# Light token groups as whole alternative slot bodies, and a later output table, in an attention + mixture-of-experts kernel

## The chip, the core and the metric

The kernel runs on one core of a Trainium2 chip. The metric is the device time of one execution in microseconds (us). The engines are called by the names the profile uses: PE (TensorE, matrix products), DVE (VectorE), ACT (ScalarE), POOL (GpSimd), and SP (SyncE, which issues most of the DMA transfers). Each engine has its own instruction stream; streams meet at semaphores.

## What is computed

Three stages follow each other. The reference, cut to what matters:

```python
attn = softmax(mask(q @ k.T / 8))            # batch 2, 12 heads, 448 positions, head size 64, causal
x    = merge_heads(attn @ v)                 # 896 tokens x 768
logits = unit(x) @ unit(expert_emb).T / tau  # 8 experts; one expert per token (argmax)
for e in range(8):                           # w1[e]: 768x1024, w2[e]: 1024x768
    h = relu(x[mask_e] @ w1[e])
    out[mask_e] = gate[mask_e] * (h @ w2[e])
h = maximum(maximum(out @ W1, out @ W2), out @ W3)   # three 768x768 matrices
y = h @ w_out                                        # 768x768
```

How many tokens fall to each expert is known only while the kernel runs. With the inputs that are timed the eight counts are 58, 5, 0, 109, 283, 0, 96 and 345.

## The kernel before, in words

**Stages.** Attention runs until about 122 us of the profiled execution. Routing is mixed into the end of attention: DVE counts the tokens of each expert, and small matrix products turn the counts into places. Then come the expert slots, up to 12 of them. A *heavy* slot computes 128 tokens of one expert (operands are split into a high and a low half in fp32r, and high by high, high by low and low by high are multiplied). With the counts above there are seven heavy slots, 0 to 6: expert 4 in slots 0 and 1, expert 6 in slot 2, expert 7 in slots 3, 4 and 5, expert 3 in slot 6. What is left of an expert (at most 64 tokens) is a *light* group; it is computed beside a heavy slot that needs no new weights, as a rider. Here expert 4's rest (27 tokens) rides in slot 3, expert 0's 58 in slot 4, expert 1's 5 in slot 6. Slot 5 has no rider. After the slots come the product with three matrices and maximum (345 to 471 us), then the output product (to 514 us), whose rows are scattered by an indirect DMA with the index table `sidx`.

**A slot.** `slot(i)` issues, on PE: L1 (768 to 1024, halves `l1[0]`, `l1[1]`), the transposes of the previous slot's result (`ytr`), transposes of the hidden layer (`htr`), L2 in four pieces, and the transposes of the next slot's gathered tokens (`xnext`). Interleaved with these, `S.ws` splits the next slot's weights: ACT casts the raw tile to the high half (L250), DVE subtracts for the low half (L251), both inside `tc.If(self.need > 0)`, since only a change of expert needs it. The raw tiles are DMAs on SP (768 KB each, six buffers). Slots 1, 2 and 5 prepare a new expert's weights.

**Tables.** The placement of the light groups is worked out on DVE with small operations: `lights1` (placed in slot 0 by a written order, the token `lt1`), `lights2` and `lights3` (between the routing and the middle of slot 1), then `light_gates` and `sorted_table` (in slot 1, the token hook `(1, 0)`), which builds the one-hot operand for the 16 small products `ix` that PE does at the end of slot 1, and `sidx`. The integer table `tabi` holds what the engines load into registers: offsets, whether weights are new, the number of slots (T_N), and for each light group its size, expert and offset.

**A light rider.** `Light` has five parts (`x`, `L1`, `hT`, `L2`, `out`), each in units of 32 tokens. Every unit stands in a conditional block of its own on every engine (`tc.If(self.n > 32 * u)` at L410, `tc.If(self.n > 0)` at L402 and L416), nine conditional blocks for each slot from 3 on. L1 uses four column tiles of 32 (one per 256 of the 1024 columns), L2 three of 32.

**Control.** Slots 3 to 11 are nested in `tc.If(nslot > i)` (L1212). `mark_branch_hint_location` at the end of a slot tells PE, POOL and SP ahead of time which way the next of these tests will go. Behind the nest stands a second test for tail groups (`ntail`, L1217), whose body is jumped over here.

## Time and profile before

| | us |
|---|---|
| three timed runs | 522.18, 525.52, 525.69 |
| median | 525.52 |
| profiled execution | 521.98 |
| its span (first to last instruction) | 520.3 |

| stretch of the profiled execution | from | to |
|---|---|---|
| attention, routing | 0 | 122 |
| slot 0, slot 1 (start of its L1) | 122 | 142.8 |
| slot 1 | 142.8 | 172.4 |
| slot 2 | 173.0 | 195.3 |
| slot 3, with a rider of 27 tokens | 195.3 | 225.6 |
| slot 4, with a rider of 58 tokens | 225.6 | 263.0 |
| slot 5, no rider | 263.0 | 290.3 |
| slot 6, with a rider of 5 tokens | 290.3 | 325.2 |
| no PE work | 325.2 | 334.9 |
| three matrices, maximum | 334.9 | 471 |
| output product and last stores | 471 | 520.3 |

Slot boundaries are the first L1 product of each slot on PE. PE is busy for 90% of the span, so a view is read by asking where PE idles and who ends that idle time. "PEclk" in a row is the TensorE clock that was granted, as a share of full speed.

### The profile page before, as it was taken

The page shows a single profiled execution, that of the slowest core. Times are in us where ns is not written, and L with a number is a line of the kernel's source. Part 1 is how long each engine was busy: PE and PEld are TensorE (multiplying, and loading weights), DVE is VectorE, ACT ScalarE, POOL GpSimd, SP SyncE. Part 2 cuts the span into 40 slices and gives each one's busy share as a digit, 9 for nine tenths or more (in the row PEclk, how much of TensorE's full clock was granted, in tenths as well). Part 3 has the DMA queues.
Part 4 walks back from the last instruction along what each step waited for, and adds up shares of the span by engine and source line. Part 5 has one row for each costly group of instructions (what it writes and reads, how often), then busy time and mean ns, then how long its engine had stood idle before and what let it go on. Part 6 is the DMA issues. An engine that isn't in the chain of part 4 may idle for free. (4 is left out here: it accounts for less than half of the span.)

```text
span 520.3 us, 9113 instructions
## 1 busy us (share of the span) xinstructions
PE 470.7 (90%) x2968; PEld 396.9 (76%) x2968; DVE 310.9 (60%) x707; ACT 236.9 (46%) x521; POOL 47.7 (9%) x80
## 2 busy tenths in 40 slices
PE   7999999998795899989987789299999999999995
PEld 6756666776785698777876568289999999999994
DVE  5898878985769875101014711269998898941000
ACT  6668679895454485122043631253444444321000
POOL 5321121110101020100001000000000000000111
PEclk9999999999897799999999789699999999999998
DMA  8645239610266699682416953643443550000111
GB/s 226 213 126 142 78 91 371 225 37 19 61 227 248 235 330 350 230 325 68 149 61 186 398 197 129 245 186 118 170 142 118 181 174 9 1 0 31 62 60 61
DMA packets 28652, 81.72 MB, mean 157 GB/s; under 512 B 13432, under 2 KB 14968, under 8 KB 28576
## 3 DMA queue, kind: packets, MB, share of 16 engines
q1 hardware_dynamic: 25648, 71.46, 39.3%
q0 software_dynamic: 2304, 9.24, 5.3%
q8 instruction: 31, 0.51, 0.4%
q14 instruction: 45, 0.37, 0.2%
q10 hardware_dynamic: 624, 0.14, 0.2%
HBM read 75.33 MB, written 5.51 MB: 155 GB/s over the span
## 5 line engine op out<-in xcount | busy, mean ns | idle before, releaser
L1177 PE MATMUL pm<-x2h,dwl 128*128 128x448 f32 x204 | 74.7, 366 | 0.0
L1176 PE MATMUL pm<-x2l,dwh 128*128 128x448 f32 x204 | 74.7, 366 | 0.0
L1175 PE MATMUL pm<-x2h,dwh 128*128 128x448 f32 x204 | 74.6, 365 | 0.0
L622 PE MATMUL pss<-kt,qbd 128*128 128x320 f32 (+6 forms) x168 | 45.7, 395 | 0.9 <-ACT prb L636 0.6
L1181 PE MATMUL l<-w2h,hh 128*128 128x384 f32 x112 | 41.1, 367 | 3.3 <-PEq L410 2.2
L636 ACT ACTIVATE prb<-pss,sm 128x64 f32<-128x64 f32 (+6 forms) x84 | 39.5, 483 | 9.6 <-DVE sm L629 9.4
L251 DVE TENSOR_TENSOR w1l<-raw,w1h 128x768 fp32r<-128x768 f32 x24 | 21.8, 953 | 34.6 <-ACT w1h L250 30.5
L1181 PE MATMUL l<-w2l,hh 128*128 128x384 f32 x112 | 39.2, 350 | 2.9 <-DVE w2l L270 2.9
L1176 PEld LDWEIGHTS pm<-x2l,dwh 128*128 128x128 f32 x204 | 38.3, 188 | 3.3
L1175 PEld LDWEIGHTS pm<-x2h,dwh 128*128 128x128 f32 x204 | 38.3, 188 | 3.3
L1177 PEld LDWEIGHTS pm<-x2h,dwl 128*128 128x128 f32 x204 | 38.3, 188 | 3.3
L183 ACT CAST dwh<-dt_t 128x768 fp32r<-128x768 f32 (+1 forms) x20 | 15.5, 773 | 48.0 <-DVE dt_t L182 48.0
L1181 PE MATMUL l<-w2h,hl 128*128 128x384 f32 x112 | 28.4, 357 | 9.7 <-DVE hl L213 5.6
L1181 PE MATMUL l<-w1h,xhp 128*128 128x512 f32 x73 | 33.1, 453 | 3.6 <-ACT w1h L250 1.5
L622 PEld LDWEIGHTS pss<-kt,qbd 128*128 128x128 f32 x168 | 28.1, 190 | 9.3 <-issue 1.7
L629 DVE TENSOR_REDUCE sm<-pss 128x1 f32<-128x448 f32 (+6 forms) x84 | 31.4, 412 | 4.6 <-PE pss L625 4.4
L1181 PE MATMUL l<-w1l,xhp 128*128 128x512 f32 x73 | 31.6, 433 | 0.0
L656 PE MATMUL pst<-ident,prb 128*128 128x128 f32 x192 | 30.0, 281 | 1.8 <-DVE prb L646 1.4
L1181 PEld LDWEIGHTS l<-w2h,hl 128*128 128x128 f32 x112 | 21.4, 199 | 10.5 <-DVE hl L213 6.0
L1177 PE MATMUL po<-woh,h2l 128*128 128x384 f32 (+2 forms) x84 | 28.1, 335 | 0.0
L1176 PE MATMUL po<-wol,h2h 128*128 128x384 f32 (+2 forms) x84 | 28.1, 334 | 0.0
L1175 PE MATMUL po<-woh,h2h 128*128 128x384 f32 (+2 forms) x84 | 28.1, 334 | 0.0
(329 smaller groups left out, 953.4 us busy)
## 6 DMA issues: line engine op xcount, KB each, us to landing
raw<-in_moe_w_dram SPq DMA_DIRECT2D x56, 768.0 KB, 6.5
rawd<-in_moe_w_dram SPq DMA_DIRECT2D x18, 768.0 KB, 4.4
rawd<-in_moe_w_out_dram SPq DMA_DIRECT2D x6, 768.0 KB, 4.2
vr<-in_v_dram SPq DMA_DIRECT2D x12, 256.0 KB, 2.8
kt<-in_k_dram SPq DMA_DIRECT2D x12, 224.0 KB, 3.5
xd<-xall POOLq DMA_DIRECT2D x12, 224.0 KB, 3.3
qbd<-in_q_dram SPq DMA_DIRECT2D x23, 112.0 KB, 4.1
xrp<-xd,idx POOLq DMA_INDIRECT x8, 7.4
```

Source lines behind the costliest of these rows:

```text
L183: nc.scalar.copy(out=hi[:, c0:c1], in_=f)
L251: nc.vector.tensor_tensor(out=lo[:, sl], in0=r[:, sl], in1=hi[:, sl], op=ALU.subtract)
L622: nc.tensor.matmul(ps[:, o:o + n], lhsT=qbd[p % 4][:, i], rhs=ktt[p][:, :n], start=i == SG[g][0], stop=False, skip_group_check=True)
L629: nc.vector.tensor_reduce(out=sms[p][:, 0, SC[i]:SC[i] + 1], in_=held["s", p, g][:, SO[i]:SO[i] + 64 * (i + 1)], axis=AX.X, op=ALU.max, ne ...
L636: nc.scalar.activation(out=prb[p % 2][:, poff[i]:poff[i] + n], in_=ps[:, SO[i]:SO[i] + n], func=AF.Exp, bias=sm[:, 0, SC[i]:SC[i] + 1], sc ...
L656: nc.tensor.transpose(ps[:, n * P:(n + 1) * P], prb[p % 2][:, poff[i] + kt * P:poff[i] + (kt + 1) * P], ident)
L1175: nc.tensor.matmul(o, lhsT=lh, rhs=rh, start=first, stop=False)
L1176: nc.tensor.matmul(o, lhsT=lh, rhs=rl, start=False, stop=False)
L1177: nc.tensor.matmul(o, lhsT=ll, rhs=rh, start=False, stop=last)
L1181: nc.tensor.matmul(o, lhsT=a, rhs=b, start=first and n == 0, stop=last and n == len(ops) - 1)
```

## The change

Six things are changed together.

1. A slot from 3 on is one of three whole bodies, chosen by a number `kind` (two bits for each slot in one register): no rider, a rider of up to 32 tokens, a rider of up to 64 tokens. Each body is straight: the rider's parts have no conditional blocks of their own, and a body with a rider has no weight preparation.
2. The rider's shapes: 32 tokens use four column tiles of 32 in L1 and in L2, 64 tokens two column tiles of 64 in both.
3. The placement tables have fewer DVE operations. `lights1` becomes `lights` and stands later (behind `qh1` in the written order); `lights2` and `lights3` become one `lights2`, which stands in slot 2 behind the last split of w1 and ahead of those of w2. `light_bases` (two operations) follows at the end of slot 2. `light_gates` is gone.
4. At the end of slot 2 every engine loads T_KIND into a register.
5. The tail groups are tested ahead of the slots 3 to 11, with a hint, instead of behind them; the hints for the next slot's test are now also given to ACT and DVE, in bodies with a rider, from the test of slot 4 on.
6. `sorted_table` and its 16 products stand behind the three-matrix stage.

The diff, cut to these parts:

```diff
     class Light:
-        def __init__(self, s, raw_of=None):
...
-        def units(self, part):
-            for u in range(2):
-                with tc.If(self.n > 32 * u):
-                    part(u)
+        def __init__(self, row, nt):
+            self.row, self.nt, self.T = row, nt, P // nt
+            self.w = {}
...
+            self.load([(0, p) for p in (0, 2, 1, 3)])
+            nc.gpsimd.tensor_copy(out=lix, in_=idx[:, bass.ds(self.e + NH, 1)])
+            nc.gpsimd.indirect_dma_start(out=lxr[:nt], out_offset=None, in_=xd, in_offset=bass.IndirectOffsetOnAxis(ap=lix[:nt], axis=0))
+            nc.gpsimd.tensor_copy(out=lgt, in_=grep[:, self.T // 4, bass.ds(self.e, 1)])
+            self.load([(1, p) for p in (0, 2)])
...
         def L1(self):
+            T, f = self.T, 1024 // self.T
+            for k in range(KD):
+                for t in range(T):
+                    n, c0 = divmod(t * f, 512)
+                    w = self.w[0, 2 * n + k // 3].rearrange("p (k f) -> p k f", k=3)
+                    self.mm(pb, self.xT[:, k], w[:, k % 3, c0:c0 + f], k, t, f, k == KD - 1)
...
     def slot(i, prep, prev):
         S = Slot(i, prep)
         S.begin()
         S.regs()
-        R = S.rider = Light(i, S.raw_of) if i > 2 else None
+        if i < 3:
+            slot_body(S, prev, None)
+            return S
+        kind = (rest["k"] // 4 ** (i - 2)) % 4
+        with tc.If(kind == 0, preferred_fallthrough_block=True) as plain:
+            slot_body(S, prev, None)
+        with plain.Else():
+            with tc.If(kind == 1, preferred_fallthrough_block=True) as small:
+                slot_body(S, prev, Light(i - 2, 32))
+            with small.Else():
+                slot_body(S, prev, Light(i - 2, 64))
+        return S
...
+    def kinds_load():
+        rest["k"] = nc.values_load(tabi[0:1, T_KIND:T_KIND + 1], min_val=0, max_val=4 ** NL * (NT + 1) - 1)
...
-    hooks = {(1, 0): sorted_table, (1, 1): lambda: (sorted_table2(), rest_load())}
-    for i in range(3, NH):
+    hooks = {(1, 1): rest_load, (2, 1): lambda: (light_bases(), kinds_load())}
+    for i in range(4, NH):
         hooks[i - 1, 0] = lambda i=i: rest_hint(i, ET.PE, ET.Pool, ET.SP)
+        hooks[i - 1, 2] = lambda i=i: rest_hint(i, ET.Activation, ET.DVE)
+    hooks[2, 0] = lambda: lights2()
+    hooks[2, -1] = lambda: tc.mark_branch_hint_location("tail0", 0, engines=(ET.PE, ET.Pool, ET.SP))
+    hooks[2, 2] = lambda: tc.mark_branch_hint_location("tail0", 0, engines=(ET.Activation, ET.DVE))
...
-    lights2()
-    lights3()
     slot_mid(S1)
     prev = slot(2, True, S1)
     nslot, olast = rest["n"], rest["o"]
     with ExitStack() as es:
+        for t in range(NT):
+            es.enter_context(tc.If(rest["k"] >= 4 ** NL * (t + 1), preferred_fallthrough_block=True, label=f"tail{t}"))
+            L = Light(NL + t, 64)
+            for part in (L.begin, L.x, L.L1, L.hT, L.L2, L.out):
+                part()
+    with ExitStack() as es:
         for i in range(3, NH):
             es.enter_context(tc.If(nslot > i, preferred_fallthrough_block=True, label=f"rest{i}"))
             prev = slot(i, i + 1 < NH, prev)
-    ntail = nc.values_load(tabi[0:1, T_LN + NH:T_LN + NH + 1], min_val=0, max_val=64)
-    with tc.If(ntail > 0, preferred_fallthrough_block=False):
...
+    table = sorted_table()
     for t in range(N // P):
...
+        if t == 0:
+            sorted_table2(*table)
```

**How the order moves.** On DVE in slot 1, before, the last rows of `lights3` and the first split of slot 1 (`w1l`) stand like this:

```order
L96 TENSOR_TENSOR lxw<-enT,tabf 128x160
L99 TENSOR_REDUCE base<-lxw 128x8 [waits DVE_49]
L1146 COPY tabf<-base 1x12
L96 TENSOR_TENSOR tabf<-one 1x1
L1148 CAST tabi<-tabf 1x12 [waits DVE_49]
L1149 CAST tabi<-tabf 1x81 [waits DVE_49]
L368 COMPARE_AND_BRANCH
L251 TENSOR_TENSOR w1l_72<-raw,w1h_71 128x768 [waits DMAHW4_49,Activation_49]
```

The same place in the changed kernel, from the split of the hidden layer (`hl`) that precedes those rows:

```order
L372 UNCONDITIONAL_BRANCH [waits DVE_49]
L221 TENSOR_TENSOR hl<-htp,hh 128x512 [waits Activation_49]
L326 TENSOR_LOAD tabi
L372 COMPARE_AND_BRANCH
L253 TENSOR_TENSOR w1l_72<-raw,w1h_71 128x768 [waits DMAHW4_49,Activation_49]
```

Nothing stands between `hl` and the first `w1l` now but a register load and the test. The operations went to slot 2; on DVE their last rows stand there, ahead of the splits of w2 (`w2l`):

```order
L100 TENSOR_REDUCE tabf<-d_1701 128x1 [waits DVE_49]
L1146 CAST tabi<-tabf 1x56 [waits DVE_49]
L1147 CAST tabi<-base 1x10
L372 COMPARE_AND_BRANCH
L253 TENSOR_TENSOR w2l_1248<-raw,w2h_1247 128x768 [waits DMAHW0_49,Activation_49]
```

The first CAST to `tabi` writes, among others, T_KIND. On PE the end of slot 2 in the changed kernel, up to the first test of the tail groups:

```order
L1187 MATMUL l_1744<-w2h_1253,hl 128x384 x4
L372 UNCONDITIONAL_BRANCH
L1195 TENSOR_LOAD tabi [waits DVE_49]
L1222 COMPARE_AND_BRANCH
L409 MATMUL lxt<-ident,lxw 128x64 [waits DMASW0_49,DVE_49]
```

PE loads T_KIND there and waits for DVE first; then comes the test that jumps over the tail groups (whose first rows are the last one shown), the test of slot 3 and the test of its kind. Where a body with a small rider ends on PE, the changed kernel has:

```order
L450 MATMUL lyt<-ident,hp_91 64x128 [waits Activation_49]
L450 MATMUL lyt<-ident,hp_91 64x128 x2
L467 UNCONDITIONAL_BRANCH
L1187 MATMUL l_3245<-w1h_71,xhp 128x512 [waits Activation_49]
```

The unconditional branch leads past the body for 64 tokens, whose first row is the last one shown.

## Rows read from the trace of the kernel before

**Rows 1.** Timeline of DVE, slot 0: start, duration, instruction, [idle before <- releaser].
```profile
132.82 0.15 DVE L96 TENSOR_TENSOR fl<-nbs 128x8 f32<-128x8 f32 x1
...
136.47 2.69 DVE L270 TENSOR_TENSOR w2l<-raw,w2h 128x768 fp32r<-128x768 f32 x3
...
149.28 0.22 DVE L1055 COPY gx<-px 128x60 f32<-128x60 f32 x1 [3.19 <-PE px L988]
```

**Rows 2.** Timeline of PE, slots 0 to 2.
```profile
137.48 0.44 PE L1181 MATMUL l<-w2l,hh 128*128 128x384 f32 x1 [2.89 <-DVE w2l L270]
...
164.50 1.65 PE L1181 MATMUL l<-w2h,hl 128*128 128x384 f32 x4 [5.64 <-DVE hl L213]
...
172.41 0.59 PE L983 MATMUL ix<-pay,lhT 112*128 112x7 bf16 x16 [2.27 <-DVE lhT L96]
...
176.14 0.63 PE L1181 MATMUL l<-w1l,xhp 128*128 128x512 f32 x1
176.57 0.63 PE L1181 MATMUL l<-w1h,xhp 128*128 128x512 f32 x1
...
180.69 0.40 PE L1181 MATMUL l<-w1l,xhp 128*128 128x512 f32 x1
180.93 0.40 PE L1181 MATMUL l<-w1h,xhp 128*128 128x512 f32 x1
```

**Rows 3.** Timeline of DVE, slots 1 and 2.
```profile
151.96 0.17 DVE L1079 SCALAR_TENSOR_TENSOR v<-nbs,n8p 128x8 f32<-128x8 f32 x1
...
160.28 3.56 DVE L251 TENSOR_TENSOR w1l<-raw,w1h 128x768 fp32r<-128x768 f32 x4
...
194.19 6.16 DVE L251 TENSOR_TENSOR w2l<-raw,w2h 128x768 fp32r<-128x768 f32 x7
```

**Rows 4.** Stretches by engine: busy (instructions) for PE, PEld, DVE, ACT, POOL; PEclk.
```profile
152.00:172.40 20.40, 12.50 (x65) 11.72 (x63) 19.44 (x58) 13.12 (x21) 1.55 (x2) 0.82 0.73 272
172.40:195.30 22.90, 22.63 (x120) 19.86 (x121) 18.24 (x25) 14.58 (x24) 2.82 (x3) 0.86 0.79 280
...
290.20:325.20 35.00, 31.44 (x226) 25.74 (x226) 10.95 (x15) 11.88 (x20) 0.00 (x0) 0.88 0.59 225
```

**Rows 5.** Groups of PE, slots 3 to 6: busy, mean ns | idle before; light L2, light L1.
```profile
L456 PE MATMUL ll<-raw,lhT 128*32 128x256 f32 (+1 forms) x256 | 15.3, 327 | 0.7 <-ACT hp L458 0.6
...
L428 PE MATMUL ll<-raw,y 128*32 128x256 f32 x192 | 11.2, 381 | 0.6 <-ACT hp L431 0.6
```

**Rows 6.** Timeline of PE in attention: products on 64 columns of the array.
```profile
113.27 2.10 PE L674 MATMUL psa<-pt,vr 128*64 128x448 f32 x16
```

**Rows 7.** Waits of PE, 195 to 335 us: who for whom, total, times, longest.
```profile
PE l L1181 <- issue: 2.5, 1, 2.5
PE ytp L294 <- ACT y L289: 2.3, 1, 2.3
PE l L1181 <- PEq L410: 2.2, 4, 0.8
PE xtp L225 <- PEq L410: 2.0, 3, 0.9
PE l L1181 <- ACT w1h L250: 1.5, 1, 1.5
PE l L1181 <- ACTq L410: 1.2, 1, 1.2
...
PE lht L441 <- DVE lhT L442: 0.6, 1, 0.6
...
PE lyt L467 <- ACT x2T L469: 0.5, 1, 0.5
```

**Rows 8.** Timeline of ACT at the end of the slots.
```profile
334.33 2.90 ACT L212 CAST x2h<-x2T 128x448 fp32r<-128x448 f32 x6 [8.66 <-issue]
```

**Rows 9.** Timeline of PE, same place.
```profile
334.94 0.74 PE L1181 MATMUL pm<-x2h,dwh 128*128 128x448 f32 x1 [9.76 <-ACT x2h L212]
```

**Rows 10.** The chain of waits in order of time, same place.
```profile
329.73 3.99 issue
```

## The prediction

> **What bounds the kernel now.** PE is busy for most of the span, so I read its timeline and waits first, and looked up for each idle stretch who ended it. Before slot 3 PE idles three times for DVE: 2.89 us, 5.64 us and 2.27 us [rows 2]. The DVE timeline says why. In slot 0 the operations of `lights1` stand from 132.82 to 136.47, ahead of the `w2l` that PE wants [rows 1]. In slot 1 `lights2` and `lights3` stand from 151.96 to 160.28, ahead of four `w1l` [rows 3], behind which comes the `hl` that PE waits for [rows 2]. The sorted table delays the 16 `ix` products, whose own 0.59 us also lie in PE's path [rows 2]. DVE was busy for 19.44 us of the 20.4 us of slot 1, so there it sets the pace [rows 4].

> Idle time costs twice. [...] The granted clock was 0.82 of full speed in slot 1 and 0.86 in slot 2 [rows 4].

> From slot 3 on, many waits end at PE's own sequencer or at "issue", that is, at branches: four of up to 0.8 us, three of up to 0.9, one of 2.5 [rows 7]. Waits on ACT's `y` (2.3) and `w1h` (1.5) also stand there [rows 7]. At the end of the slots PE idles for 9.76 us until ACT has made `x2h` [rows 9], and ACT had waited 8.66 us for nothing but issue [rows 8]; one piece of the chain there is 3.99 us of issue [rows 10]: far jumps over the bodies that are not run.

> **The change part by part**, in order of time. The sum is made against the profiled execution (521.98 us, span 520.3), which is 3.5 us under the median of 525.52.

> *Slots 0 and 1.* The waits 2.89, 5.64 and 2.27 and the 0.59 us of `ix` go: 11.4 us. In slot 1 the next limit is PE's own work: no later `w1l` or `hl` has another wait ahead of it than ACT. With the waits go stretches at the lower level; 0.18 of 20.4 us is 3.7 us of lost clock, but most of it lies inside the idle time, so I take 2 us (bounds 0 and 3.7). `lights` moves into DVE's idle 3.19 us before `gx` [rows 1]; its 20 operations at 0.18 us (8.3 us over the some 45 of `lights2` and `lights3`, first and last in [rows 3]) are 3.7 us, so 0.5 to 0.8 us come back as delay. Gain 12.6 us: slot 2 starts at 160.4 instead of 173.0.

> *Slot 2.* PE took 22.3 us, 2.7 of them by the lower level (14 products at 0.19 us more [rows 2]); 19.6 remain, and PE ends at 180.0. But all engines then wait for T_KIND. The last `w1l` ended at 194.19 [rows 3], 21.2 us into the slot, so 18.5 now: 178.9. Behind it come the 23 operations of the new `lights2`: 0.18 us each are 4.2 us; two are wider than the mean, and I take 5.3 (upper bound: the old 8.3). The kinds are ready at 184.3 and PE has waited 4.3 us. Behind PE's register load stand the hinted jump over the tail groups and, for slot 3's rider, the far jump over the plain body; no other PE work can pass them.

> *What a jump costs.* No row shows these jumps. The nearest are jumps over a skipped light block, 0.4 to 0.9 us [rows 7], the 2.5 us issue of one far jump on PE [rows 7] and 3.99 us on ACT [rows 10]. I take 2.9 us for a far jump without a hint (nearer to PE's row) and 1.3 for the hinted one (between 0.9 and 2.5); bounds 0.7 and 4.0. [...]

> So slot 3 starts at 184.3 + 0.3 (load) + 1.3 + 2.9 = 188.8, against 195.3: 6.5 us of the 12.6 are left. PE will have idled for 9 us, so I add 2.7 us of lower clock in slot 3.

> *Slot 3.* A rider of 32 tokens: L1 unchanged at 11.2/4 = 2.8 us [rows 5]. L2 was 15.3/4 = 3.8 us on three uneven column tiles; the same columns on four even tiles, at the rate of L1 (48 instructions of 256 columns in 2.8 us), are 64 of 192 columns: 2.8 us. Gain 1.0, and 1.0 of waits at conditional blocks. At its end PE makes three far jumps: past the 64-token body, and over the plain and the small body of slot 4. That is 8.7 us; I let 1.5 us lie beside work still queued: 7.2. The wait of 1.2 us that opened slot 4 goes [rows 7]. Net 2.7 − 2.0 + 7.2 − 1.2 = +6.7: the lead is used up at 226.

> *Slot 4.* 58 tokens took two units: 2 × 2.8 and a wait of 0.6 for L1, 2 × 3.8 and 0.6 for L2 [rows 5], 14.4 in all. On two tiles of 64 the instructions halve (24 of 512 columns, 32 of 384). The nearest rows: `psa`, 64 columns of the array, 0.131 us for 448 columns [rows 6], gives 3.6 us for each; a full-width product (0.24 us for 512 columns [rows 2]) gives 5.6. I take 4.5 for each: 5.4 gained (bounds 3.2 and 7.2). The waits at `lht` (0.6) and `lyt` (0.5) [rows 7] go, 1.7 us of lower clock come. No jump follows: this body is the last of the three, and slot 5's is the first. Gain 4.8.

> *Slot 5.* The waits at light blocks (0.9, 0.6, 0.8), the 2.5 of issue and the 1.5 on `w1h` go: 6.3. Its end jumps over both rider bodies, and slot 6 over its plain one: 5.8 − 1.5 = 4.3 come, and 1 us of lower clock goes. Gain 3.0.

> *Slot 6.* L2 1.0; the waits of 2.3 (`y`), 0.6 and 0.4: 4.3 gained, and 1.3 of lower clock (0.88 of full speed now [rows 4], 4 us lost, against 2.7 taken). Gain 5.6.

> *End.* ACT now makes one far jump (2.9) and one with a hint (1.3) before `x2h`, whose first cast is 0.6: with half a microsecond of issue 5.3 us instead of 9.76. Gain 4.5.

> *Output.* `ix` puts 0.6 us into PE's path. The table's DVE work, some 3 us, lies beside the last products, where DVE has little to do; without that cover it would cost those 3 us.

> Sum: 6.5 (lead at slot 3) − 6.7 + 4.8 + 3.0 + 5.6 + 4.5 − 0.6 = 17.1 us. On the profiled execution 504.9, on the median 508.4. I say **506**.

> **Rivals.**
> *Jumps dearer than they gain* (slower). Seven far jumps lie in PE's path, 17.3 us in my sum, which would be a gain of 34.4 without them: from 4.9 us each the change loses. At 6 us each and a further 1.7 us of lower clock behind four of them it is 506 + 25 (42 in place of 17.3) + 7 = 538. For it: ACT's stop of 8.66 us held two [rows 8]. Against: 3.99 us is the longest single piece seen [rows 10]. [...]
> *The wait for the kinds returns the early gain.* If `lights2` needs its old 8.3 us, or the rider's gather, which POOL now issues behind the kinds and jumps, ends after PE wants its transposes, slot 3 starts near 192 or stops later: 509 to 515.
> *Jumps nearly free*, at 0.9 us, as over skipped blocks [rows 7]: 11 us less (7 × 0.9 in place of 17.3), and some 4 us less of lower clock: about 491.
> *The early gain is not there*, because slot 1's raw weights come no sooner on the DMA queue and `w1l` waits for them: half of 12.6 is lost, but the wait for the kinds stays: 512.

> Chances: forecast (499 to 511) 0.50; the kinds 0.17; the DMA 0.08; jumps nearly free 0.14; dearer jumps 0.11, of which 0.07 end above 531 and 0.04 within 1% of before (about what can be told from no change). The range, 493 to 518, leaves out the dearer jumps and the far end of the cheap ones. With mixtures of the cases that end within 1%: faster 0.81, same 0.12, slower 0.07.

> **What would show it.** On PE no waits on DVE near slot 0's `w2l`, slot 1's `hl` and `ix`; slot 2's first product near 160. Idle time of some 9 us ahead of slot 3, of 7 ahead of slot 4, of 4 ahead of slot 6, none ahead of slot 5, all ended by issue or by PE's sequencer. One `ll` group of 4.5 us in slot 4. Some 5 us between the last rider and `pm`. I am wrong if slot 3 starts after 192, if a far jump shows under 1 or over 4 us, or if the light products at 64 tokens take over 5.6 us.

## The result and the profile after

The changed kernel takes 506.91 us (median of four runs, 505.45 to 508.82), the kernel before 524.31 us beside it. The ratio is 0.967, with a 95% interval of 0.962 to 0.973: faster. The forecast was 506 us, in a range from 493 to 518. The profiled execution took 505.45 us, with a span of 503.7.

The stages, from the first products of the slots on PE. "Forecast" is the term of the prediction for the same stretch.

| stretch | before, us | after, us | change | forecast |
|---|---|---|---|---|
| up to the start of slot 2 | 173.0 | 158.8 | −14.2 | −12.6 |
| slot 2 and the wait ahead of slot 3 | 22.3 | 26.3 | +4.0 | +6.1 |
| slot 3 and the idle time ahead of slot 4 | 30.3 | 39.6 | +9.4 | +6.7 |
| slot 4 | 37.5 | 33.8 | −3.7 | −4.8 |
| slot 5 and the idle time ahead of slot 6 | 27.2 | 23.1 | −4.1 | −3.0 |
| slot 6 | 34.9 | 29.9 | −5.0 | −5.6 |
| idle time ahead of the three matrices | 9.8 | 5.8 | −4.0 | −4.5 |
| the rest | 185.4 | 186.4 | +1.1 | +0.6 |
| sum | 520.3 | 503.7 | −16.6 | −17.1 |

The timeline of PE after, rows at the slots' borders (start, duration, instruction, idle time before and its releaser), which answer to [rows 2], [rows 7] and [rows 9]:

```profile
158.78 0.39 PE L1187 MATMUL l<-w1h,xhp 128*128 128x512 f32 x1
...
185.09 0.79 PE L1187 MATMUL l<-w1h,xhp 128*128 128x512 f32 x1 [6.99 <-DVE w2l L253]
...
224.73 0.77 PE L1187 MATMUL l<-w1h,xhp 128*128 128x512 f32 x1 [11.08 <-issue]
...
258.54 0.48 PE L1187 MATMUL l<-w1h,xhp 128*128 128x512 f32 x1
...
281.63 0.78 PE L1187 MATMUL l<-w1h,xhp 128*128 128x512 f32 x1 [4.07 <-ACT y L291]
...
317.28 0.74 PE L1187 MATMUL pm<-x2h,dwh 128*128 128x448 f32 x1 [5.77 <-ACT x2h L214]
```

The three waits of PE for DVE in slots 0 and 1 are gone, and the first products of slot 2 start 0.23 us apart at a granted clock of 1.00 (158.78 to 162.0); before, they started 0.43 us apart [rows 2] at 0.50 (173.0 to 177.0). In their place are four long stops, ahead of slots 3, 4 and 6 and at the end. Between them only two small ones stand, 0.43 us in slot 3 and 0.99 in slot 6. Slot 5 follows slot 4 without a gap.

The DVE timeline of slots 1 and 2 answers to [rows 3]; `lights2` runs from the row at 176.84 to the CAST at 180.51 that writes T_KIND:

```profile
150.26 3.56 DVE L253 TENSOR_TENSOR w1l<-raw,w1h 128x768 fp32r<-128x768 f32 x4 [1.64 <-ACT w1h L252]
153.75 0.68 DVE L215 TENSOR_TENSOR hl<-htp,hh 128x512 fp32r<-128x512 f32 x1
...
176.84 0.45 DVE L97 TENSOR_TENSOR lxw<-enT,v 128x288 f32<-128x288 f32 x1
...
180.51 0.18 DVE L1146 CAST tabi<-tabf 1x56 int32<-1x56 f32 x1
180.61 0.15 DVE L1147 CAST tabi<-base 1x10 int32<-1x10 f32 x1
180.74 7.04 DVE L253 TENSOR_TENSOR w2l<-raw,w2h 128x768 fp32r<-128x768 f32 x8
```

DVE now has time left in slot 1 (it waits 1.64 us for ACT), and T_KIND is written from 180.51 on, 2.4 us after PE's last product of slot 2 ends (178.1). The light products of slot 4, timeline of PE:

```profile
240.68 5.37 PE L414 MATMUL ll<-raw,y 128*64 128x512 f32 x24
...
250.78 5.38 PE L414 MATMUL ll<-raw,lhT 128*64 128x384 f32 x32
```

What fills most of the stops are PE's own jumps. The view of one source line lists the branches too (engine queue, operation, count, then minimum, median and maximum in ns, first and last start). L464 is the test for a plain body, L467 that for a small one and the jump out of it, L372 here the jump behind a plain body, and L1228 the test for the next slot. In order of time, ahead of slot 3, of slot 4 (two lines), of slot 6 (two) and at the end (two):

```profile
L464 PEldq COMPARE_BRANCH  x1: 2505/2505/2505, 182.2 to 182.2; - x1
...
L464 PEldq COMPARE_BRANCH  x1: 4432/4432/4432, 212.5 to 212.5; - x1
...
L467 PEldq COMPARE_BRANCH  x2: 386/3861/7336, 211.7 to 217.2; - x2
...
L372 PEldq COMPARE_BRANCH  x1: 6217/6217/6217, 274.3 to 274.3; - x1
...
L464 PEldq COMPARE_BRANCH  x1: 235/235/235, 280.9 to 280.9; - x1
...
L467 PEldq COMPARE_BRANCH  x1: 3411/3411/3411, 309.5 to 309.5; - x1
...
L1228 PEldq COMPARE_BRANCH  x2: 203/1798/3392, 313.0 to 316.6; - x2
```

At 182.2 PE jumps over the plain body of slot 3: 2.51 us. At 211.7 PE leaves the small body of slot 3, past the body for 64 tokens: 0.39 us. At 212.5 it jumps over the plain body of slot 4: 4.43 us. At 217.2 it jumps over the small body: 7.34 us. The jump behind slot 5's body (past both rider bodies) takes 6.22 us, for 3.3 of which PE still had queued work; the one over slot 6's plain body takes 0.24 us; at the end of slot 6 the jump past the body for 64 takes 3.41 us, the next one, out of the nest, 3.39. So the same kind of jump costs from 0.2 to 7 us.

The trace also shows the transfers of instructions, in a DMA queue of their own. In the stop ahead of slot 4 (213.6 to 224.7 us) the queue q8 moved three of them, 16 KB each:

```profile
q8 instruction: 3, 0.05, 2.3%
```

### The profile page after: what moved, and what is told of

It is laid out like the page before. It is cut to its first block, busy times and chain, and to the rows that moved or that the text cites. A ratio compares the mean times of both kernels' runs of the same rounds, so it can differ in the third digit from the quotient of the medians.

```text
span 503.7 us, 8299 instructions
## 1 busy us (share of the span) xinstructions
PE 460.2 (91%) x2801; PEld 384.7 (76%) x2801; DVE 304.6 (60%) x697; ACT 235.9 (47%) x521; POOL 54.9 (11%) x98
## 5 line engine op out<-in xcount | busy, mean ns | idle before, releaser
L1187 PE MATMUL l<-w1h,xhp 128*128 128x512 f32 x73 | 33.7, 462 | 23.1 <-issue 12.1
L215 DVE TENSOR_TENSOR hl<-htp,hh 128x512 fp32r<-128x512 f32 x11 | 7.6, 689 | 57.0 <-ACT hh L214 48.1
L1187 PEld LDWEIGHTS l<-w1h,xhp 128*128 128x128 f32 x73 | 16.1, 220 | 26.3 <-issue 18.6
L1333 POOL DMA_INDIRECT out_dram<-ob,sidx x7 | 6.8, 977 | 209.3 <-DVE sidx L1178 177.6
L1187 PE MATMUL l<-w2h,hl 128*128 128x384 f32 x112 | 26.9, 344 | 2.0 <-DVE hl L221 2.0
```

Source lines behind the costliest of these rows:

```text
L215: nc.vector.tensor_tensor(out=lo, in0=ps_ap, in1=hi, op=ALU.subtract)
L1187: nc.tensor.matmul(o, lhsT=a, rhs=b, start=first and n == 0, stop=last and n == len(ops) - 1)
L1333: nc.gpsimd.indirect_dma_start(out=out, out_offset=bass.IndirectOffsetOnAxis(ap=sidx[:, t:t + 1], axis=0), in_=ob, in_offset=None)
```

## The experiments

Each is an edit of the changed kernel, save e6, and is timed against the kernel before. "After" below is the changed kernel.

**e1: fewer weight transfers at the jump.**

```diff
-                self.w[kind, p] = wraw()
-                wdma(self.e, kind, p, self.w[kind, p])
+                if (kind, 0) not in self.w:
+                    self.w[kind, 0] = wraw()
+                    wdma(self.e, kind, p, self.w[kind, 0])
+                self.w[kind, p] = self.w[kind, 0]
```

> The changed kernel with one thing left out: a rider loads one raw tile of w1 and one of w2 and uses it in all four places (2 transfers of 768 KB in place of 8; the riders' results are thus not the reference's). Theory (PE's far jumps fetch their target through the same DMA engines as the weights, and wait behind the rider's weight transfers): the 11.1 us of idle PE between slots 3 and 4 fall to 5 to 7 us, since the jump over the small body no longer meets busy DMA engines; the jump at the end of slot 6 (3.4 us on quiet engines) stays; in all 4 to 7 us faster than the changed kernel. Rival (a far jump costs what it costs, by its distance): the idle time stays at 10 to 12 us, and the time stays within 2 us of the changed kernel's.

Measured: 503.67 us, ratio 0.960 (0.956 to 0.964). While PE stood ahead of slot 4, the DMA engines were busy for 0.93 of the time in after. Here is that stretch of after (last three numbers: granted clock, DMA share, GB/s), then from e1 PE's first product of slot 4 (timeline) and the jumps ahead of it (by source line):

```profile
213.65:224.73 11.08, 0.00 (x1) 0.03 (x1) 0.00 (x0) 1.98 (x6) 0.37 (x2) 0.63 0.93 350
```

```profile
223.88 0.76 PE L1189 MATMUL l<-w1h,xhp 128*128 128x512 f32 x1 [9.09 <-issue]
```

```profile
L466 PEldq COMPARE_BRANCH  x1: 4015/4015/4015, 213.6 to 213.6; - x1
...
L469 PEldq COMPARE_BRANCH  x2: 291/3052/5812, 212.9 to 217.9; - x2
```

The stop shrinks by 2.0 us, between the two expectations. The jump over the small body still takes 5.8 us with most of the transfers gone (7.3 in after). During that jump the DMA engines were busy for 0.30 of the time, in after for all of it. Two other runs, e3 and e7, change nothing on PE and have stops of 11.85 and 10.98 us there, so 2.0 us are clear of the scatter. The weight transfers lengthen a jump, but they are the smaller part of it. My theory held in kind and failed in size.

**e2: one taken jump per slot.**

```diff
-        with tc.If(kind == 0, preferred_fallthrough_block=True) as plain:
-            slot_body(S, prev, None)
-        with plain.Else():
-            with tc.If(kind == 1, preferred_fallthrough_block=True) as small:
+        with tc.If(kind < 2, preferred_fallthrough_block=True) as few:
+            with tc.If(kind == 0, preferred_fallthrough_block=True) as plain:
+                slot_body(S, prev, None)
+            with plain.Else():
                 slot_body(S, prev, Light(i - 2, 32))
-            with small.Else():
-                slot_body(S, prev, Light(i - 2, 64))
+        with few.Else():
+            slot_body(S, prev, Light(i - 2, 64))
```

> The tests are nested the other way: kind < 2 (plain or small) first, the body for 64 in the outer else. Slot 4 then makes one taken jump over the plain and the small body in place of two in a row. Theory (each taken far jump is a fetch of its own, one after the other): the idle time between slots 3 and 4 falls from 11.1 us by one jump, 3 to 5 us; slots 3 and 6 (one taken jump each, as now) stay within 1 us; in all 3 to 5 us faster. Rival (the fetches wait for the weight transfers, and one fetch ends when those are done, however many jumps): the idle time falls by less than 2 us.

Measured: 501.95 us, ratio 0.956 (0.952 to 0.960). The first product of slot 4 (timeline), and the jump over both bodies at once (by source line):

```profile
224.76 0.77 PE L1187 MATMUL l<-w1h,xhp 128*128 128x512 f32 x1 [6.28 <-issue]
```

```profile
L464 PEldq COMPARE_BRANCH  x1: 5932/5932/5932, 218.7 to 218.7; - x1
```

The stop falls from 11.08 to 6.28 us, and the medians differ by 5.0 us. One jump of 5.9 us stands for two of 4.4 and 7.3, although it is the longer one: these jumps are paid each for itself, not by their distance.

**e3: the kinds sooner, within slot 2.**

```diff
-    hooks[2, 0] = lambda: lights2()
-    hooks[2, -1] = lambda: tc.mark_branch_hint_location("tail0", 0, engines=(ET.PE, ET.Pool, ET.SP))
+    hooks[2, -1] = lambda: (lights2(), tc.mark_branch_hint_location("tail0", 0, engines=(ET.PE, ET.Pool, ET.SP)))
```

> The 23 operations of lights2 move within slot 2, from behind the last four w1l to ahead of the xlp and these w1l. Theory (PE waits for the kinds, which are ready 3.9 us of DVE work after the last w1l): the kinds are ready some 4.5 us sooner than now, before PE ends slot 2, and the idle PE time ahead of slot 3 falls from 7.0 us to the load and the jumps alone, 4.0 to 4.5; slot 3's products wait for no w1l, as the last four are for its second half; 2 to 3 us faster. Rival (the jump over the plain body, not the kinds, is what ends last, or w1l is late in its place): the idle time stays at 6 to 7 us or a wait of PE on w1l of 1 to 3 us appears in slot 3, and the time stays within 1 us.

Measured: 508.37 us, ratio 0.971 (0.966 to 0.976). The wait ahead of slot 3 falls even to 2.56 us, yet the time does not follow: the expected gain of 2 to 3 us is not there. PE's stops in slot 3:

```profile
180.97 0.49 PE L1187 MATMUL l<-w1h,xhp 128*128 128x512 f32 x1 [2.56 <-ACT w2h L252]
...
190.20 1.54 PE L296 MATMUL ytp<-ident,y 128*128 128x128 f32 x6 [2.85 <-ACT y L291]
...
198.25 0.53 PE L409 MATMUL lxt<-ident,lxw 32*128 32x32 f32 x6 [3.17 <-issue]
```

The gain is given back at `y` and at the rider's transposes. PE's wait for ACT's `y` ends at 190.20 here. In after ACT starts `y` at 189.34, having waited 6.93 us until DVE, with eight `w2l` to do ahead of it, has passed the test of the tail groups. The rider's tokens come by POOL's gather (L395). Timeline of POOL, the first two rows from e3, the last from after:

```profile
178.72 9.63 POOL L313 COPY glast<-gs 128x1 f32<-128x1 f32 x1 [21.52 <-DMA xrp<-xd,idx]
...
189.94 0.89 POOL L395 DMA_INDIRECT lxw<-xd,lix  x1 [0.27 <-POOL lix L394]
...
189.28 0.90 POOL L395 DMA_INDIRECT lxw<-xd,lix  x1 [3.20 <-DVEq L1222]
```

In after the gather waits, like `y`, until DVE has passed the test of the tail groups: that branch starts at 189.0 and the gather at 189.28. DVE's last operation ahead of the test ends at 188.44 there and at 188.68 in e3, no sooner, for its work in slot 2 is the same; so the gather could hardly have started before 189.5 in e3 (an estimate, by the 0.84 us between that end and the gather in after). A copy of one column, which took 0.64 us in after, also takes 9.63 here, and ends (188.35) when DVE's run of `w1l` and `w2l` does (177.53 to 188.0); it accounts for the 0.4 us or so that remain. Neither theory had this.

**e4: a hint for the kind.**

```diff
+    def kind_hint(i):
+        tc.mark_branch_hint_location(f"plain{i}", (5 - (rest["k"] // 4 ** (i - 2)) % 4) // 5, engines=(ET.PE,))
...
-        hooks[i - 1, 0] = lambda i=i: rest_hint(i, ET.PE, ET.Pool, ET.SP)
+        hooks[i - 1, 0] = lambda i=i: (rest_hint(i, ET.PE, ET.Pool, ET.SP), kind_hint(i))
```

The tests of the kinds also get the labels that the hints name.

> A hint is added on PE, behind the hint for the next slot's test: the jump over the next slot's plain body, taken or not by its kind. Theory (a jump's cost is the fetch of its target, which a hint starts early): the first of the two jumps ahead of slot 4 (4.4 us) falls under 1 us, the second (7.3 us, no hint) stays; slot 6's jump over its plain body is cheap already (0.2 us); slot 3's has no hint; at the end the later hint may undo the earlier one. In all 2 to 4 us faster. Rival (the hint of the next test and that of the kind share one place, or fetching early only meets other weight transfers): no change within 2 us, or 1 to 2 us lost at the end of slot 6.

Measured: 512.50 us, ratio 0.979 (0.975 to 0.983), slower than after. The jumps ahead of slot 4:

```profile
L464 PEldq COMPARE_BRANCH  x1: 240/240/240, 217.5 to 217.5; - x1
...
L467 PEldq COMPARE_BRANCH  x2: 6008/6705/7402, 211.1 to 218.2; - x2
```

The hinted jump fell from 4.43 to 0.24 us, as the theory had it. But the jump out of the small body, which lies ahead of it, rose from 0.39 to 6.01 us, slot 6's jump over its plain body from 0.24 to 3.28, and the one out of the nest from 3.39 to 4.84. That the hint had taken the place of what was fetched for the nearer jump would explain all three; it was not tried by itself. There is a rival: the hint adds instructions to PE's code and so moves all that lies behind them. e10 below has no new hint, only moved code, and there the same two jumps rise alike, that out of slot 3's body to 5.9 us and that over slot 6's plain body to 4.7. So the fall of the hinted jump is likely the hint's doing (in e10 it costs 6.75 us behind an equally dear first jump), but the rises cannot be put down to it.

**e5: the conditional blocks again, all of them entered.**

```diff
+        def rp(part):
+            with tc.If((rest["k"] // 4 ** (i - 2)) % 4 > 0):
+                part()
...
-            R.L1()
+            rp(R.L1)
+            R.load2()
```

`x`, `hT`, `L2` and `out` get the same; `load2` issues the loads that stood at the end of `L1`.

> The changed kernel with each of the rider's five parts (x, L1, hT, L2, out) put back into a conditional block of its own, whose test is always true where it runs; nothing else is changed. Theory (a conditional block stops each engine's run-ahead, some 0.5 us each where PE feels it): waits of 0.3 to 0.9 us at four or five of the parts come back in slots 3, 4 and 6, 5 to 9 us in all, and the time rises by that. Rival (in the kernel before these waits only stood in for the wait on ACT or DVE that ends there anyway): under 2 us.

Measured: 504.12 us, ratio 0.960 (0.952 to 0.969), not to be told from after; one of the four runs took 510.40 us, and the other three, which the ratio rests on, 502.09 to 505.97. The waits of PE in this kernel, 170 to 320 us, are the stops at the slots' borders alone; at the five parts there is nothing but 0.69 us at `lxt` in slot 3. So no wait of PE shows at a block that is entered. The seven waits on PE's sequencer in [rows 7] lie in slots 3, 5 and 6, where blocks were jumped over (slot 5 had no rider, and 27 and 5 tokens need one unit of two), and none in slot 4, where both units ran.

**e6: the end alone, in the kernel before.**

```diff
-    for i in range(3, NH):
-        hooks[i - 1, 0] = lambda i=i: rest_hint(i, ET.PE, ET.Pool, ET.SP)
+    for i in range(4, NH):
+        hooks[i - 1, 0] = lambda i=i: rest_hint(i, *ALLE)
+    hooks[2, 0] = lambda: tc.mark_branch_hint_location("tail0", 0, engines=ALLE)
```

The load and the test of `ntail` and its body also move ahead of the nest of slots 3 to 11, as in after.

> The kernel before with part 5 alone: the test of the tail groups stands ahead of slot 3, with a hint for all engines, and the hints for the next slot's test go to ACT and DVE too. Theory (the 9.76 us at the end were two far jumps on ACT, one after the other): the idle PE time at the end falls to 5 to 6 us, or less with ACT's hint; ahead of slot 3 one hinted jump and a load come, 1 to 2 us; in all 2 to 4 us faster than before. Rival (the end waits for something else, such as PE's own jump): the idle time at the end stays above 8 us, and the time stays within 1 us of before or is above it.

Measured: 524.40 us, ratio 1.001 (0.997 to 1.005): no change. The end did what was expected, and more (PE, then POOL in slot 3):

```profile
210.14 0.87 PE L418 MATMUL lxt<-ident,lxw 64*128 64x64 f32 x6 [4.24 <-issue]
...
337.52 0.47 PE L1181 MATMUL pm<-x2h,dwh 128*128 128x448 f32 x1 [2.96 <-ACT x2h L212]
```

```profile
198.17 5.64 POOL L404 DMA_INDIRECT lxw<-xd,lidx  x1 [5.95 <-DVE w2l L251]
```

The stop at the end fell from 9.76 to 2.96 us. In return slot 3 took 37.2 us in place of 30.3: POOL issued the rider's gather only at 198.17, in 5.64 us, where the kernel before needed 0.91, and again DVE's eight `w2l` (195.99 to 203.0) ran beside it. The wait on `y` in slot 6 also rose, from 2.30 to 6.03 us, while the 2.49 us of issue in slot 5 went. So the saving at the end is real, and in this kernel something else gives it back.

**e7: `lights2` ahead of the middle of slot 1.**

```diff
-    hooks[2, 0] = lambda: lights2()
...
+    lights2()
     slot_mid(S1)
```

> The changed kernel with lights2 (23 operations, 3.9 us of DVE) back at its place before the middle of slot 1; the kinds are still loaded at the end of slot 2. Theory (DVE sets the pace of slot 1 and has only some 1.6 us to spare there): slot 2 starts 2 to 3 us later, with a wait of PE on hl in slot 1 and the lower clock behind it; the wait for the kinds goes, but ACT and DVE enter slot 3 no sooner than their work in slot 2 ends, so slot 3's start is given back in waits on y and on the rider's transposes; the time is 0 to 3 us above the changed kernel's. Rival (the wait for the kinds is what costs): 2 to 4 us faster than the changed kernel.

Measured: 502.29 us, ratio 0.958 (0.952 to 0.964), 4.6 us below after by the medians, above the 2 to 4 that the rival expected. The rival was right. PE in slots 1 and 3:

```profile
155.47 0.97 PE L1187 MATMUL l<-w2h,hl 128*128 128x384 f32 x4 [1.14 <-DVE hl L215]
...
181.72 0.79 PE L1187 MATMUL l<-w1h,xhp 128*128 128x512 f32 x1 [3.58 <-ACT w2h L252]
```

In slot 1 the 3.9 us of DVE work cost PE 1.14 us, since DVE had 1.64 to spare there. Ahead of slot 3 the stop falls from 6.99 to 3.58 us, and slot 3 then runs for 28.6 us as in after: nothing is given back, because DVE's `w2l` and the entry of DVE, ACT and POOL into slot 3 move forward as well. That is the difference from e3, where only the order within slot 2 changed. Of the 5.4 us between the two profiled executions 3.4 lie ahead of slot 3. Most of the rest lies in slot 4 and ahead of slot 6, where this edit does nothing; the stop ahead of slot 6 is 2.66 us in place of 4.07.

**e8 and e9: both gains, and the load sooner.** e8 is e2 with e7. In e9 also:

```diff
-    hooks = {(1, 1): rest_load, (2, 1): lambda: (light_bases(), kinds_load())}
+    hooks = {(1, 1): lambda: (rest_load(), kinds_load()), (2, 1): lambda: light_bases()}
```

> The two edits that gained, together: the nest with one taken jump per slot, and lights2 back before the middle of slot 1. Theory (the two gains lie at different places, 4.8 us ahead of slot 4 and 3.4 us ahead of slot 3, and nothing later gives them back): 497 to 500 us, 7 to 9 us under the changed kernel. Rival (they share a cause, or the place of the code moves other jumps): 501 to 504.

> As e8, and the register load of the kinds moves from the end of slot 2 to the end of slot 1, so that no engine loads or waits there. Theory (what is left ahead of slot 3 in e7, 3.6 us, is the jump over the plain body and ACT's work, not the load): within 1 us of e8. Rival (the load and its wait are on the path): 1 to 2 us faster than e8.

Measured: e8 497.28 us, ratio 0.949 (0.945 to 0.953); e9 499.31 us, ratio 0.952 (0.949 to 0.955). The gains of e2 and e7 add (5.0 and 4.6 against 9.6). PE in e8, ahead of slots 3, 4 and 6 and at the end:

```profile
184.21 0.79 PE L1187 MATMUL l<-w1h,xhp 128*128 128x512 f32 x1 [4.29 <-ACT w2h L252]
...
219.36 0.76 PE L1187 MATMUL l<-w1h,xhp 128*128 128x512 f32 x1 [6.50 <-issue]
...
274.99 0.79 PE L1187 MATMUL l<-w1h,xhp 128*128 128x512 f32 x1 [3.40 <-ACT w2h L252]
...
310.95 0.74 PE L1187 MATMUL pm<-x2h,dwh 128*128 128x448 f32 x1 [5.85 <-ACT x2h L214]
```

e9 gains nothing over e8: it is 2.0 us slower by the medians, with intervals that overlap, and its stop ahead of slot 3 is 3.60 us, as in e7. No sign shows that the load was on the path.

**e10 to e12: code that never runs.**

```diff
             for part in (L.begin, L.x, L.L1, L.hT, L.L2, L.out):
                 part()
+            if t == 0:
+                pb = bank("h", "lht", 1)
+                for _ in range(64):
+                    nc.tensor.transpose(pb[:, :P], hp0[:, :P], ident)
```

This is e10. e11 and e12 add 32 and 96 of these products to e8.

> The changed kernel with 64 more products in the body of the first tail group, which is jumped over in every run: no engine executes anything more, but all later code of PE lies some half a block of the instruction queue (16 KB transfers in the profile) further on. Theory (a jump is cheap where its target lies in what is already fetched, and costs a transfer or two where not, so its price hangs on where the code lies): single jumps change by 2 to 4 us in either direction (the free one at the end of slot 3 becomes dear, or the 7.3 us one cheaper), the sum by up to 5 us. Rival (a jump's price hangs on its length alone): every idle stretch of PE stays within 1 us, and the time within 1 us.

> As e8, with 32 products (half of e10's padding) in the body of the first tail group, which never runs. Theory (the place of the code sets which targets are already fetched): single jumps of PE change by 2 to 4 us against e8, and the sum falls between 492 and 505 us; what direction cannot be told ahead. Rival (e10's 5 us were the longer jump over the tail groups or chance): every idle stretch within 1 us of e8's, 496 to 499 us.

> As e11, with 96 products. The same theory and rival: single jumps 2 to 4 us off those of e8 and e11, the sum between 492 and 505 us, against 496 to 499 us with every idle stretch within 1 us.

Measured: e10 511.82 us, ratio 0.976 (0.972 to 0.980), 4.9 us above after; e11 504.48 us, ratio 0.962 (0.957 to 0.968), 7.2 us above e8; e12 496.88 us, ratio 0.949 (0.943 to 0.954), as e8. In e10 the first product of slot 4 (timeline), the jumps ahead of it and, last, the tests for the plain bodies of slots 5 and 6 (by source line):

```profile
233.95 0.77 PE L1187 MATMUL l<-w1h,xhp 128*128 128x512 f32 x1 [17.95 <-issue]
```

```profile
L464 PEldq COMPARE_BRANCH  x1: 6747/6747/6747, 220.6 to 220.6; - x1
...
L467 PEldq COMPARE_BRANCH  x2: 5905/6024/6142, 214.2 to 227.6; - x2
...
L464 PEldq COMPARE_BRANCH  x2: 66/2384/4701, 265.5 to 287.6; - x2
```

The free jump out of slot 3's body has become one of 5.9 us, and the stop is 17.95 us in place of 11.08. Slot 6's jump over its plain body has risen from 0.24 to 4.7 us. The jump over slot 6's plain body and the one at its end, in e8 (two lines) and in e12 (two lines):

```profile
L465 PEldq COMPARE_BRANCH  x1: 232/232/232, 274.7 to 274.7; - x1
...
L465 PEldq COMPARE_BRANCH  x1: 3292/3292/3292, 303.1 to 303.1; - x1
...
L465 PEldq COMPARE_BRANCH  x1: 3401/3401/3401, 273.8 to 273.8; - x1
...
L465 PEldq COMPARE_BRANCH  x1: 442/442/442, 302.9 to 302.9; - x1
```

In e12 the first has become dear and the second cheap: the sums are alike by chance. In e11 the stops ahead of slots 4 and 6 are 10.95 and 7.12 us, where e8 has 6.50 and 3.40; from these I take the jumps behind slot 3's body and ahead of slot 6 to be dear there. No instruction of these kernels is executed that e8 or after did not execute. The place of the code alone moves the time by up to 7 us. The nest of e2 gains in both cases: with a cheap jump out of slot 3's body the stop ahead of slot 4 is 11.08 us in after and 6.28 in e2, with a dear one 17.95 in e10 and 10.95 in e11.

## Why the prediction was right, and where it was not

**Slots 0 and 1: right.** The three waits and `ix` went, with the lower clock behind them (0.82 in slot 1 before [rows 4], 1.00 now): 14.2 us against 12.6. Of the two small terms, 2 us of clock had an upper bound of 3.7, and the 0.5 to 0.8 us of delay from `lights` did not show as a wait of PE. No run takes this part alone; the rows of before and after are what shows it.

**Slot 2 and the kinds: the mechanism right, the size off by 2.1 us.** The 23 operations took 3.9 us, not 5.3; 0.17 us each, so the lower bound was the better value. What follows the kinds took 4.4 us, forecast 4.5; its parts were other ones: the hinted jump over the tail groups took 0.39 us, not 1.3, the jump over the plain body 2.5, not 2.9, and the tests between them the rest. e7 shows that the wait was a true cost and not a cover for something else. The lower clock behind a stop, 2.7 us in slot 3 and 1.7 in slot 4, was an estimate. In after the granted clock was 0.58 from 185.09 to 190.0 and 0.50 from 224.73 to 230.0; 10 and 12 products there started some 0.43 us apart, where 0.23 is usual later, which makes 2.0 and 2.5 us (an estimate from these starts).

**What a jump costs: the step that was off.** One price of 2.9 us was put on all far jumps. They cost from 0.2 to 7.3 us, and the three ahead of slot 4 made a stop of 11.1 us where 7.2 were forecast. The bounds of 0.7 and 4.0 were too narrow on both sides, and by the prediction's own sign (a far jump under 1 or over 4 us) its price was wrong. Its two sources were not what they were taken for: in the 2.5 us of issue in slot 5 [rows 7] no branch of PE stands (those near it took up to 0.33 us), but an instruction transfer of q8; and the seventh of the "seven far jumps in PE's path" is ACT's, at the end. The errors partly cancelled: the jump out of slot 3's body and that over slot 6's plain body were nearly free. e1 puts some 2 us of the excess down to the weight transfers that share the DMA engines; e2 shows that two jumps in a row are paid twice; e10 to e12 show that which jumps are dear hangs on where the code lies. The jumps of after fall into two classes, of 0.2 to 0.4 us without a transfer of q8 within them and of 2.5 us and more with one. Those over plain bodies stand in both: 2.5, 4.4 and 0.2 us. So that the median came out within 1 us of the forecast is luck: the stretches ahead of slots 2 and 3 were 3.7 us better than forecast and slots 3 and 4 3.8 us worse, and moving code that never runs shifts the sum by more than that.

**Light products on two tiles: too low.** 5.4 us for each, not 4.5; the full-width product's rate (5.6) was the better neighbour, `psa` [rows 6] the worse one. The gain was 14.4 − 10.8 = 3.6 us, not 5.4. On four tiles the L2 of 32 tokens took 2.81 us, forecast 2.8.

**Conditional blocks: right in sum, wrong in kind.** They cost where they are jumped over, not where they are entered (e5).

**The end: 5.8 us, forecast 5.3, for another reason.** I put it down to ACT's jumps. In after PE itself was late: its two jumps of 3.4 us fill the time, and ACT, with jumps of its own behind it, waits the last 1.25 us for PE's second one. The hint for the last test brought nothing there: PE's jump out of the nest took 3.39 us, against 1.34 in before. In after the jump out of the body lies between hint and test; in e6, where no such jump does, the stop is 2.96 us. That this is the reason is likely, but was not tried by itself.

**The output: 1.1 us, forecast 0.6.** The table's DVE work was covered, as forecast.

The rival that "the wait for the kinds returns the early gain" was true in part (4.0 of 14.2 us, and the jump's share is in it). That jumps are dearer than they gain was nearer than its chance of 0.11 said: e10, with nothing but its code moved, has already lost 4.9 of the 17 us.

## What to carry to other kernels

Here straight alternative bodies traded many small stops at skipped blocks (0.4 to 0.9 us [rows 7]) for four long ones, most of them at far jumps (4.1 to 11.1 us), so count the taken jumps per path and nest the tests so that each path takes as few as possible; judge such a change by several placements of its code, since one placement can be worth 7 us of 500. A value that all engines must load before they branch belongs in a stretch where the engine that makes it has time to spare, not behind its last piece of work (e7: 4.6 us). A saving at one place counts only when the next engine to arrive there moves forward as well: e3 and e7 remove the same wait, and only e7 gains.

## What was not expected of the hardware

**POOL can stand while DVE subtracts.** A copy of one column took 9.63 us (e3) and the issue of an indirect DMA 5.64 us (e6) beside DVE's run of `w1l` and `w2l`, where 0.18 and 0.9 are usual. The copy ended 0.3 us behind DVE's run, the issue 0.8 us behind it. It is not always so. POOL in after, all three rows beside DVE's `w2l` of 180.74 to 187.78:

```profile
182.84 0.64 POOL L313 COPY glast<-gs 128x1 f32<-128x1 f32 x1 [23.98 <-DMA xrp<-xd,idx]
183.64 1.51 POOL L209 DMA_INDIRECT xrp<-xd,idx  x1 [0.15 <-issue]
185.15 0.93 POOL L394 COPY lix<-idx 128x1 int32 x1
```

These are lengthened by some 0.5 to 0.8 us each and not held to the run's end; a copy in slot 6 was (3.96 us beside the `w2l` there). What decides between the two was not tried.

**A jump's price.** On PE in after 0.2 to 0.4 us in the cheap cases; 2.5 to 3.4 us where the DMA engines were quiet (0.03 to 0.06 busy, ahead of slot 3 and at the end of slot 6); 4.4 to 7.3 us where weight transfers ran (0.70 and more); 5.8 in e1 at 0.30. The cheap jump out of slot 3's body ran while the DMA engines were 0.96 busy: in after a dear jump has a transfer of q8 and a cheap one has none, and among the dear ones the price is higher where the DMA engines are busier. ACT's branches at the same places are recorded with under 0.1 us each, but that is not their price: behind the one at 183.1 ahead of slot 3 ACT's next instruction stands 2.1 us later.

**A hint can take a far jump's price away.** The hinted jump over the eight tail groups took 0.39 us on PE in after. In e4 the hinted jump, the second of two in a row, fell by 4.2 us. The first rose by 5.6 us in the same run; that the hint did this is not shown, since moved code alone did the like (e10).
